# Loading and turning the gate row, the second key weights and the warm-up at the start of a gated attention/MLP kernel

## The chip, the cores and the metric

The kernel runs on one core of a Trainium2 chip. Times are device microseconds of one execution. A NeuronCore has five engines with a queue each: TensorE (PE, matmuls; PEld is its weight load), VectorE (DVE), ScalarE (ACT), GpSimd (POOL) and SyncE (SP). ACT, POOL and SP also issue loads and stores, which 16 DMA engines carry out.

## What is computed

For a sequence of 2048 tokens of width 576, a gate mixes a linear attention block with an MLP:

```python
x = A_x
g = _sigmoid((x * gate_w).sum(-1, keepdims=True))
a = _A_ref(x, A_wqkv, A_wo)      # 32 heads of 18; phi(t) = where(t > 0, t + 1, exp(t)) + 1e-6
b = _B_ref(x, B_w1, B_b1, B_w2, B_b2)   # layernorm, 4608 wide GELU MLP
return g * a + (1 - g) * b
```

In `_A_ref`, queries, keys and values are projections of x; phi of keys and values are summed over the sequence per head, and phi of the queries reads that sum.

## The kernel before

All matmuls keep fp32 precision by splitting each operand into a hi part (rounded to the matmul type, written by ACT with a Copy) and a low part (what is left, a subtraction on DVE), and adding the products of hi and low. The 2048 tokens lie in 16 blocks of 128. Attention comes first (some 290 us), then the MLP in chunks.

The change lies in the start, which prepares the first three blocks. PE first runs `WARM` fp32 matmuls of a tile of ones into bank 7 (line 152; each becomes two instructions). The loads are written in a fixed order (lines 430 to 444): `load_x` brings a transposed block of x by SP, one load of 256 KB and two of 32 KB; `load_w` brings one of the four halves (key or query, first or second 288 columns) of the projection weights, five pieces of 128 rows, the first four together as a main load and the fifth (64 rows) twice, as the tail. The first half of the key weights is issued by ACT in three loads, its tail by SP; everything after by SP. ACT also issues two loads of the gate row `gw`.

A half projection (`first_keys`, `first_queries`) is 14 matmuls in the order `HI_FIRST`: four hi by hi, four low x by hi weights, the two of the tail, four hi x by low weights. `split_x` and `split_w` write the parts. The gate row must become a column: five one-row transposes with the identity `ident` into bank 7 (`column`), and a DVE copy into column 288 of the second key weights, which have 290 columns: those weights' projection then also gives the gate's sum and x's own sum. So the second key weights can be split only after that copy. `make_identity` and the memset and selections of `mask` run on POOL, the former before all loads. `InOrder` makes each engine keep the order of the program; the program has eight semaphores for the loads of SP and ACT, so a ninth issue waits until an earlier load has landed.

The projections of keys go to banks 0 to 5, those of queries in turn to banks 6 and 7, so the third half projection of queries waits until DVE has read the first out of its bank (`phi`).

Of the kernel before, what the change touches and what calls it, by code (L numbers as in the profile page):

```python
# [17 lines left out]
P = 128  # L18
S, D, H, DH, F = 2048, 576, 32, 18, 4608
# [14 lines left out]
MOMENTS = ((0, 2), (2, 4), (4, 8), (8, 16))  # L34
EPS_PHI = 1e-6
EPS_LN = 1e-5
WARM = 6
FIRST = 3
LATE = 3
X_RING = 4  # L40
# [43 lines left out]
def raw(ap):  # L84
    return ap.bitcast(F32)
# [26 lines left out]
def tile_gated_mix(ctx: ExitStack, tc: tile.TileContext, x, xm, xe, wm, we, wvm, wve, wo, um, ue, w2, b1, b2, gw, out):  # L112
    nc = tc.nc
    pe, act, dve, pool = (InOrder(tc, e) for e in (nc.tensor, nc.scalar, nc.vector, nc.gpsimd))
# [17 lines left out]
    def load_twice(dst, src, by=sp):  # L132
        for half in range(2):
            by.dma_start(dst[half * 64:(half + 1) * 64], src)
# [15 lines left out]
    for n in range(4):  # L150
        dve.memset(low_rows[32 * n:32 * n + 32], -1.0 if n % 2 else 0.0)
    for _ in range(WARM):
        pe.matmul(ps[:, 7, :P], ones, ones, start=True, stop=True)
# [3 lines left out]
    accs = keep.tile([P, 7 * TPB * HALF], F32, name="accs")  # L157
    spare = accs[:, :7 * TPB * HALF - TPS * D]
    ident = spare[:, 25 * P:26 * P]
    make_identity(nc, ident)  # L160
    mask = spare[:GW, 26 * P:26 * P + GW]
    acc = [accs[:, spare.shape[1] + i * D:][:, :D] for i in range(TPS)]
    acc += [accrp.tile([P, D], F32, name=f"acc{i}") for i in range(TPS, NT)]
# [20 lines left out]
    QUERY, KEY = range(2)  # L184
    W, at_ = {}, 0
    for part in (KEY, QUERY):
        for half in range(2):
            n = HALF + 2 * (part == KEY and half)
# [17 lines left out]
    def load_w(part, half, pieces=((0, 5),), by=sp):  # L206
        if (part, half) not in wraw:
            wraw[part, half] = wsp.tile([P, 5, HALF + 2], F32, name="s", tag="s")
        s = wraw[part, half]
        main = wm[part * 2 + half].rearrange("p (t n) -> p t n", t=4)  # L210
        tail = we[part * 2 + half]
        for t0, t1 in pieces:
            if t0 < 4:
                by.dma_start(s[:, t0:min(t1, 4), :HALF], main[:, t0:min(t1, 4)])
            if t1 == 5:
                load_twice(s[:, 4, :HALF], tail, by)

    def split_w(part, half, by=dve, pieces=((0, 5),)):
        w = W[part, half]
        s = wraw[part, half][:, :, :w.shape[2]]  # L220
        for t0, t1 in pieces:
            act.activation(w[:, t0:t1], s[:, t0:t1], AF.Copy)
            by.tensor_tensor(out=w[:, 5 + t0:5 + t1], in0=s[:, t0:t1], in1=raw(w[:, t0:t1]), op=OP.subtract)

    def load_x(i):
        xraw[i] = yt.tile([P, 5, P], F32, name="t")
        sp.dma_start(xraw[i][:, 0:4], xm[i].rearrange("p (t n) -> p t n", t=4))
        load_twice(xraw[i][:, 4], xe[i])

    def split_x(i, pieces=((0, 5),)):  # L230
        if i not in xs:
            xs[i] = x_places[PLACE[i] % X_RING]
        to, src = xs[i], xraw[i]
        for t0, t1 in pieces:
            act.activation(to[:, t0:t1], src[:, t0:t1], AF.Copy)
            if t0 < 4:
                dve.tensor_sub(to[:, 5:9], src[:, 0:4], raw(to[:, 0:4]))
            if t1 == 5:
                dve.tensor_sub(to[64:P, 4], src[64:P, 4], raw(to[64:P, 4]))
# [12 lines left out]
    def project(i, part, half, order=BY_ROWS, n=None):  # L252
        w = W[part, half]
        p = banks[i, part, half] = ps[:, next(halves_in) if n is None else n]
        for m, (a, b) in enumerate(order):
            pe.matmul(p[:, :w.shape[2]], xs[i][:, a, :], w[:, b], start=(m == 0), stop=(m == len(order) - 1))
# [173 lines left out]
    first = ORDER[:FIRST]  # L430
    gwr = spare[0:1, :5 * P]
    load_x(first[0])
    load_w(KEY, 0, ((0, 1), (1, 2), (2, 4)), act)
    act.dma_start(gwr[:, :D], gw.rearrange("(a n) -> a n", a=1))
    act.dma_start(gwr[:, D:], gw[4 * P:D].rearrange("(a n) -> a n", a=1))
    act.activation(tiny, ones[:, 0:1], AF.Exp)
    load_w(KEY, 0, ((4, 5),))
    load_x(first[1])
    load_w(KEY, 1)
    load_x(first[2])  # L440
    load_w(QUERY, 0)
    load_xn(first[0])
# [13 lines left out]
    def first_keys(n, half):  # L456
        project(first[n], KEY, half, HI_FIRST, 3 * half + n)
# [7 lines left out]


    column = ps[:, 7, :5]
    for t in range(5):
        pe.transpose(column[:, t:t + 1], gwr[:, t * P:(t + 1) * P], ident[0:1, 0:1])
    first_keys(0, 0)  # L470
    split_x(first[1])
    first_keys(1, 0)
    dve.tensor_copy(wraw[KEY, 1][:, :, HALF:HALF + 1], column[:, :, None])
    dve.memset(wraw[KEY, 1][:, :, HALF + 1:HALF + 2], 1.0)
    split_w(KEY, 1)
    split_x(first[2])
    load_x(ORDER[3])
    first_keys(0, 1)
# [729 lines left out]
```

## Time and profile before

| | us |
|---|---|
| runs without profile | 1133.76, 1134.5, 1137.68 |
| median of these | 1134.5 |
| the profiled execution | 1137.47 |
| its span, first to last instruction | 1135.8 |
| PE busy in the span | 1118.9 (99%) |
| DVE busy | 884.3 (78%) |
| ACT busy | 527.5 (46%) |
| POOL busy | 303.8 (27%) |
| mean granted TensorE clock | 0.997 |

The page gives busy times of one execution. A matmul's time is from its start to its modelled end, and neighbours overlap; the distance of two starts is the pace. "Idle before" names what ended an idle stretch of an engine. A name with q (SPq, ACTq) is the queue of an engine, where it issues DMAs.

### The profile page before, as it was taken

Reading aid. Unit: us, or ns where it says so; the run is one execution under the profiler, and the core shown is the slowest. Engines: PE = TensorE matmul, PEld = TensorE weight load, DVE = VectorE, ACT = ScalarE, POOL = GpSimd, SP = SyncE. Lnnn points to the kernel's source line nnn. Section 1 sums busy time; section 2 is a strip of 40 time slices with the busy share of each in tenths; the row PEclk is TensorE's granted clock in tenths of the full one; section 3 lists DMA queues with packets and bytes.
Section 4 is the critical chain, followed back from the end, with each engine's and each line's share of the span. In section 5 each row is a group of like instructions: output and inputs, shape, how many; then the busy total and the mean of one; then the engine's idle time right before and its main releaser. Section 6 shows DMA issues by size and latency. Waiting matters only on the chain.

```text
span 1135.8 us, 18099 instructions
## 1 busy us (share of the span) xinstructions
PE 1118.9 (99%) x6871; PEld 1025.1 (90%) x6871; DVE 884.3 (78%) x1354; ACT 527.5 (46%) x889; POOL 303.8 (27%) x245
## 2 busy tenths in 40 slices
PE   8999899999999999999999999999999999999998
PEld 8999899999899999999999999988999899989988
DVE  6678787798468878769778766578889888888985
ACT  4555354353545545444544544364445444544441
POOL 1011112242013122212113211234353435343520
PEclk9999899999999999999999999999999999999999
DMA  5237555334454664563764639844444444444452
GB/s 172 68 109 261 163 173 184 141 131 172 171 176 143 230 215 169 204 198 130 255 225 139 230 131 368 316 123 148 117 123 132 139 126 119 139 129 126 126 183 84
DMA packets 102861, 189.85 MB, mean 167 GB/s; under 512 B 8159, under 2 KB 58623, under 8 KB 98550
## 3 DMA queue, kind: packets, MB, share of 16 engines
q1 hardware_dynamic: 102210, 188.10, 50.4%
q8 instruction: 54, 0.88, 0.3%
q10 hardware_dynamic: 564, 0.59, 0.1%
q14 instruction: 33, 0.27, 0.1%
HBM read 121.93 MB, written 66.73 MB: 166 GB/s over the span
## 4 chain that ended last, share of the span: by engine, by line
PE 88%; DVE 6%; ACT 2%; issue 1%; DMA 1%; SPq 0%; DVEq 0%; ACTq 0%
PE ps L108 88%; DVE den L108 1%; DVE accs L108 1%; DVE qt L108 1%; DMA t<-in_xm 1%; DVE acc L108 0%; DMA yd<-ys 0%; DVE y L108 0%; DVE u L108 0%; ACT y L108 0%; DVE e L108 0%; DMA s<-in_wm 0%; DVE region L108 0%; DVE ys L108 0%; ACT h L108 0%
## 5 line engine op out<-in xcount | busy, mean ns | idle before, releaser
L108 PEld LDWEIGHTS ps<-region,h 128*128 128x128 f32 x2568 | 368.5, 188 | 22.6 <-DVE accs L108 1.0
L108 PE MATMUL ps<-region,h 128*128 128x288 f32 x2568 | 383.2, 295 | 0.5 <-DVE fresh L108 0.2
L108 PE MATMUL ps<-y,wa 128*128 128x512 f32 x1008 | 265.0, 392 | 0.0
L108 POOL TENSOR_TENSOR fresh<-fresh 128x384 f32<-128x384 f32 (+1 forms) x128 | 138.1, 1084 | 438.5 <-DMA w1d<-wb 125.9
L108 PE MATMUL ps<-y,wb 128*128 128x512 f32 x756 | 201.1, 395 | 1.0 <-ACT u L108 1.0
L108 PEld LDWEIGHTS ps<-y,wa 128*128 128x128 f32 x1008 | 177.8, 188 | 26.2
L108 DVE TENSOR_TENSOR accs<-ps,accs 128x576 f32<-128x576 f32 x210 | 158.0, 753 | 32.6 <-PE ps L108 22.9
L108 ACT ACTIVATE h<-u,b1s 128x512 fp32r<-128x512 f32 x90 | 65.2, 725 | 214.7 <-DVE u L108 214.7
L108 PEld LDWEIGHTS ps<-y,wb 128*128 128x128 f32 x756 | 132.9, 188 | 23.2 <-ACT u L108 1.7
L108 DVE SCALAR_TENSOR_TENSOR accs<-ps,omg,accs 128x576 f32<-128x576 f32 (+1 forms) x146 | 118.1, 809 | 44.0 <-PE ps L108 43.2
L108 POOL TENSOR_TENSOR u<-u 128x512 f32<-128x512 f32 x64 | 100.2, 1566 | 126.4 <-ACT u L108 122.7
L108 ACT ACTIVATE u<-ps 128x512 f32<-128x512 f32 x108 | 63.7, 590 | 150.0 <-PE ps L108 149.7
L108 PE MATMUL ps<-y 128*128 128x288 f32 (+1 forms) x896 | 128.9, 302 | 1.1 <-ACT y L108 0.4
L108 PEld LDWEIGHTS ps<-y 128*128 128x128 f32 x896 | 125.8, 193 | 3.7 <-ACT y L108 0.9
L108 DVE TENSOR_TENSOR h<-u,h 128x512 fp32r<-128x512 f32 x142 | 104.9, 738 | 27.2 <-ACT u L108 27.1
L108 ACT ACTIVATE u<-u,b1s 128x512 f32<-128x512 f32 x108 | 78.3, 725 | 54.0 <-DVE u L108 51.0
L108 DVE TENSOR_TENSOR u<-ps,u 128x512 f32<-128x512 f32 x108 | 74.2, 687 | 37.1 <-ACT u L108 23.8
L108 PEld LDWEIGHTS ps<-region 128*128 128x128 f32 x600 | 90.3, 188 | 9.0 <-ACT accs L108 0.5
L108 DVE TENSOR_TENSOR region<-fresh,region 128x576 fp32r<-128x576 f32 (+1 forms) x83 | 80.8, 973 | 20.6 <-ACT region L108 20.6
L108 PE MATMUL ps<-region 128*128 128x288 f32 x600 | 96.2, 295 | 0.1
L108 PE MATMUL ps<-wp,qt 128*128 128x288 f32 x448 | 63.6, 298 | 0.8 <-DVE qt L108 0.8
L108 PEld LDWEIGHTS ps<-wp,qt 128*128 128x128 f32 x448 | 59.9, 188 | 1.3 <-DVE qt L108 1.3
(131 smaller groups left out, 1045.8 us busy)
## 6 DMA issues: line engine op xcount, KB each, us to landing
w1d<-wa SPq DMA_DIRECT2D x18, 1280.0 KB
wa<-w1d SPq DMA_DIRECT2D x72, 320.0 KB
y<-yd SPq DMA_DIRECT2D x14, 1280.0 KB
w1d<-wb SPq DMA_DIRECT2D x18, 960.0 KB
wb<-w1d SPq DMA_DIRECT2D x54, 320.0 KB
fresh<-in_w SPq DMA_DIRECT2D x20, 576.0 KB
fresh<-in_w SPq DMA_DIRECT2D x32, 288.0 KB
fresh<-in_um SPq DMA_DIRECT2D x64, 128.0 KB
```

The source lines that it names most:

```text
L108: return lambda *args, **kwargs: self.tc.keep_in_program_order(op(*args, **kwargs))
```

## The change

`WARM` goes from 6 to 11. ACT issues, instead of the two loads of the gate row, the main load of the second key weights. POOL issues the gate row's two loads and the two tail loads of the second key weights; SP no longer issues these weights. `make_identity` is moved behind the loads of the second x block, on POOL behind its four loads. The five transposes of the gate row stand behind the first half projection instead of ahead of it. The second key weights are split in two pieces, the four main ones and the tail.

```diff
-WARM = 6
+WARM = 11
...
-    make_identity(nc, ident)
...
     load_w(KEY, 0, ((0, 1), (1, 2), (2, 4)), act)
-    act.dma_start(gwr[:, :D], gw.rearrange("(a n) -> a n", a=1))
-    act.dma_start(gwr[:, D:], gw[4 * P:D].rearrange("(a n) -> a n", a=1))
+    load_w(KEY, 1, ((0, 4),), act)
+    pool.dma_start(gwr[:, :D], gw.rearrange("(a n) -> a n", a=1))
+    pool.dma_start(gwr[:, D:], gw[4 * P:D].rearrange("(a n) -> a n", a=1))
+    load_w(KEY, 1, ((4, 5),), pool)
     act.activation(tiny, ones[:, 0:1], AF.Exp)
     load_w(KEY, 0, ((4, 5),))
     load_x(first[1])
-    load_w(KEY, 1)
+    make_identity(nc, ident)
     load_x(first[2])
...
     column = ps[:, 7, :5]
+    first_keys(0, 0)
+    split_x(first[1])
     for t in range(5):
         pe.transpose(column[:, t:t + 1], gwr[:, t * P:(t + 1) * P], ident[0:1, 0:1])
-    first_keys(0, 0)
-    split_x(first[1])
     first_keys(1, 0)
     dve.tensor_copy(wraw[KEY, 1][:, :, HALF:HALF + 1], column[:, :, None])
     dve.memset(wraw[KEY, 1][:, :, HALF + 1:HALF + 2], 1.0)
-    split_w(KEY, 1)
+    split_w(KEY, 1, pieces=((0, 4), (4, 5)))
```

## Rows read from the trace of the kernel before

**Rows 1.** The page, busy time of PE over the span.

```profile
PE 1118.9 (99%) x6871; PEld 1025.1 (90%) x6871; DVE 884.3 (78%) x1354; ACT 527.5 (46%) x889; POOL 303.8 (27%) x245
```

**Rows 2.** Chain of waits, 0 to 60 us: start, length, what.

```profile
7.87 8.07 PE ps L108 x40
...
25.51 34.61 PE ps L108 x224
```

**Rows 3.** Order of time, ACT, 0 to 17 us: start, length, operation [idle before].

```profile
2.22 2.11 ACTq L108 DMA_DIRECT2D accs<-in_gw  x2
...
4.10 0.23 ACTq L108 DMA_DIRECT2D accs<-in_gw  x1
4.36 1.28 ACT L108 ACT_TABLE_LOAD   x1 [4.36 <-DMA t<-in_xm]
...
5.76 0.61 ACT L108 ACTIVATE y<-t 128x512 fp32r<-128x512 f32 x1
...
7.15 1.00 ACT L108 ACTIVATE y<-s 128x576 fp32r<-128x576 f32 x2
8.40 0.74 ACT L108 ACTIVATE y<-t 128x640 fp32r<-128x640 f32 x1 [0.25 <-DMA t<-in_xe]
11.80 1.42 ACT L108 ACTIVATE y<-s 128x1450 fp32r<-128x1450 f32 x1 [2.65 <-DMA s<-in_we]
...
16.37 1.42 ACT L108 ACTIVATE y<-s 128x1440 fp32r<-128x1440 f32 x1
```

**Rows 4.** Order of time, SP's queue, 5 to 9 us.

```profile
6.62 0.60 SPq L108 DMA_DIRECT2D s<-in_wm  x1
7.26 1.26 SPq L108 DMA_DIRECT2D s<-in_we  x2
```

**Rows 5.** Windows of 1 us: engines' busy time, clock, DMA share, GB/s.

```profile
4.00:5.00 1.00, 0.06 (x1) 0.00 (x0) 0.00 (x0) 0.64 (x1) 0.00 (x0) 1.00 1.08 372
5.00:6.00 1.00, 0.22 (x3) 0.26 (x3) 0.00 (x0) 0.99 (x3) 0.00 (x0) 1.00 0.34 87
...
7.00:8.00 1.00, 0.83 (x3) 0.46 (x3) 0.97 (x4) 1.00 (x4) 0.00 (x0) 1.00 0.40 126
```

**Rows 6.** PE by shape in 8.3:12.8, 22:24.8, 127.5:128.9: count, busy us, mean ns.

```profile
L108 PE MATMUL ps<-y 128*128 128x288 f32 x20 | 5.2, 450 | 0.2 <-ACT y L108 0.2
...
L108 PE MATMUL ps<-y 128*128 128x288 f32 x23 | 3.2, 296 | 0.0
...
L108 PE MATMUL ps<-y 128*128 128x288 f32 x7 | 1.9, 442 | 0.0
```

**Rows 7.** Order of time, PE, 0 to 32 us: warm-up and transposes.

```profile
1.12 2.93 PE L108 MATMUL ps<-ones 128*128 128x128 f32 x12 [1.12 <-DVE ones L108]
5.78 0.71 PE L108 MATMUL ps<-accs 1*128 1x1 f32 x5 [1.72 <-DMA accs<-in_gw]
```

**Rows 8.** Order of time, DVE, 4 to 17 and 20.9 to 27 us.

```profile
9.24 1.00 DVE L108 TENSOR_TENSOR y<-t,y 128x512 fp32r<-128x512 f32 x2
10.27 0.17 DVE L108 COPY s<-ps 128x5 f32<-128x5 f32 x1
...
13.25 1.67 DVE L108 TENSOR_TENSOR y<-s,y 128x1450 fp32r<-128x1450 f32 x1 [2.80 <-ACT y L108]
...
21.83 1.55 DVE L108 TENSOR_SCALAR e<-e 128x288 f32<-128x288 f32 x1
```

**Rows 9.** Order of time, POOL, 0 to 20 us, its first work for a block.

```profile
17.55 0.67 POOL L108 COPY pks<-k 128x576 f32<-128x576 f32 x1 [15.23 <-DVE k L108]
```

**Rows 10.** One window, 122.2 to 129 us; columns as in rows 5.

```profile
122.20:129.00 6.80, 5.63 (x20) 5.25 (x21) 3.44 (x10) 1.41 (x3) 0.00 (x0) 0.50 0.31 74
```

**Rows 11.** Order of time, PE, around 123 and 148 us.

```profile
123.37 0.38 PE L108 MATMUL ps<-accs,mr 128*8 128x128 f32 x1 [3.62 <-DVE acc L108]
123.40 4.03 PE L108 MATMUL ps<-ks,xs 128*128 128x64 f32 x11
...
148.52 2.15 PE L108 MATMUL ps<-ks,xs 128*128 128x64 f32 x11
```

## Prediction of the change

> **What bounds the kernel now.** I read the page first. The profiled execution took 1137.47 us, of which 1135.8 us are span; the other 1.7 us lie outside the instructions. TensorE (PE) is busy for 99% of the span [rows 1], so a microsecond that PE gets back early stays won unless something later absorbs it. The change touches only what is issued in the first microseconds, so the second view was the chain of waits of the first 60 us [rows 2]. It runs over PE from 7.87 for 8.07 us (the first three half projections of keys, 14 matmuls each), then over ScalarE (ACT) and VectorE (DVE) to 25.51, where PE starts the third half projection of queries; from there it is PE alone for 34.61 us. What the change wins is therefore what it takes off 25.51.
>
> The third view was the order of time on each queue. ACT issues three weight loads and a gate-row load, then stands until 4.10 before the second gate-row load, begins its table load at 4.36 and the first split of x at 5.76 [rows 3]. From there to 8.15 it is never idle, so PE's start at 7.87 is set by when ACT starts, not by a load. ACT waits 0.25 us for the second x block (8.40), and 2.65 us for the second key weights (11.80). SP issues those weights late, at 6.62 to 8.52 [rows 4], while the DMA engines are half idle between 5 and 8 us [rows 5].
>
> The fourth view groups PE's matmuls by duration. In 8.3 to 12.8 us the 128x288 matmul has a mean of 450 ns, in 22 to 24.8 us 296 ns, and 442 ns in 127.5 to 128.9 [rows 6]. That last stretch has a granted clock of 0.50 [rows 10]; so the first two half projections run at the lower level (1.2 GHz) too, although the clock column shows 1.00 there. Matmuls overlap, so I count starts: 19 of the first group begin within its 4.5 us, some 240 ns apart, 21 of the second within its 2.8 us, some 135 ns apart.
>
> **The change part by part.** *ACT's queue.* The two gate-row loads leave it, with the stall before the second. In their place comes one load of 576 KB; the same load took SP 0.60 us to issue [rows 4]. ACT issued the first gate load from 2.22 [rows 3], so it is through at 2.82 instead of 4.33, and the table load (1.28 us) and the first split move 1.4 to 1.5 us earlier, to about 4.35. The first x block has landed by then: the wait that ended at 4.36 was for it. The later weight pieces are less sure; ACT never waited for them, so they are bounded only by their use (7.15 for the third piece). I take them to land by about 6.0, which gives back 0.3 us: the hi split of the third piece ends at about 6.7, and PE goes on there instead of at 7.87: 1.1 us earlier.
>
> *Warm-up.* Twelve instructions (six matmuls, two passes each) take 2.93 us [rows 7]; ten more at the 0.21 to 0.23 us of these end at about 6.2 instead of 4.05. They lie beside the loads and hold little back, since the first data comes at about 5.3 and the third weight piece at 6.7. Now PE idles from 4.05 to 5.78 [rows 7] and has gaps until 7.87, and its pace is still the slow one at 12.8 [rows 6]. Without the hole I expect the full clock by 6 to 10 us. Twenty-six matmuls at 135 instead of 240 ns would be worth 2.7 us if nothing else bound them; something does, as follows.
>
> *Gate row behind the first half projection.* Five transposes take 0.71 us of PE on either side [rows 7]. Now they lie in a gap; after, they lie on PE's path between first and second projection, but PE would wait there for the second x block anyway (below), so they cost nothing; without that wait, 0.7 us. Their copy on DVE stands behind the low split of x, as before.
>
> *Second x block, then second key weights.* This is the path that binds. Before: x landed at 8.40, its low split ended on DVE at 10.24, the column copy with its memset at 10.45 [rows 8]; the key weights came at 11.80, their hi split took 1.42 us, their low split ran from 13.25 to 14.92. After: the weights are issued from 2.2 instead of 6.6 and are there by 8 to 9. But x is issued no earlier and now shares the DMA engines with them. Bounds: not delayed at all (8.40), or by all of 576 KB at the 372 GB/s of 4 to 5 us [rows 5], 1.55 us. I take 0.3 us, near the low end, since 5 to 6 us is nearly empty (87 GB/s) and most of the weights fit before x is moved. Then low split of x until 10.55, column until 10.75, hi split of four of five pieces 1.17 us (1160 columns between the 0.43 us of 288 and the 1.42 us of 1450) until 11.9, low splits 1.36 and 0.45 us until 13.7, against 14.92. PE has used the eight products that need hi parts alone and has six left (0.8 us): the third half projection ends at about 14.5 instead of 15.94. Gain 1.2 (by DVE) to 1.4 us (by PE); I take **1.3 us**.
>
> *Splitting in two pieces* costs ACT 0.18 us and DVE 0.14 us more, and is in that sum.
>
> *From there to 25.51* nothing is changed. The split of the query weights started at 16.37 without a wait [rows 3], so they may be the next to be late; but SP now issues 1.86 us less ahead of them (0.60 and 1.26) [rows 4], more than the 1.3 us that they are wanted earlier. PE itself needs five half projections, 9.4 us, from 14.4 to 23.8: under 24.2, so DVE's chain still sets it and the 1.3 us hold.
>
> *GpSimd (POOL)* gets two gate loads and two 72 KB loads, ahead of the identity and the mask. It has nothing else to do until 17.55 [rows 9]. No row shows a load issued by POOL. Nearest rows: 0.23 us for a gate load [rows 3], 0.63 us for each half of a weight tail [rows 4], together 1.7 us; even at twice that, its few mask ops end soon after DVE's splits have begun. Beside them DVE could be held up: the 0.30 us op that took 1.55 us at 21.83 beside a POOL add shows how [rows 8]. Bounds 0 to 1.2 us; I take 0, since most of it lies ahead.
>
> Sum: 1135.8 - 1.3 = 1134.5 us span, 1136.2 us with the part outside, for an execution like the profiled one. The runs without profile took 1133.76, 1134.5 and 1137.68; against their median the forecast is 1134.5 - 1.3 = **1133.2 us**. Bounds of this case: gain 0.3 (POOL beside DVE, x later) to 1.9 us (x not later, clock early), 1132.6 to 1134.2.
>
> **The rivals.** *The clock falls at 122 us: the other side.* After a stretch of 3.62 us in which PE waits for DVE, the granted clock is 0.50 from 122.2 to 129.0 [rows 10, 11]. The eleven sums of products behind the wait take 4.03 us, and 2.15 us at 148.52 where the clock is full; until 129.0 the projection that follows runs 1.6 us at half pace, another 0.8. Together 2.7 us. The times shown lie in two pairs, 1133.8 and 1134.5, 1137.5 and 1137.7, 3.0 to 3.9 us apart; I read the upper pair as executions in which the clock fell here, as it did in the profiled one. The change neither removes nor lengthens that wait. If the median of after is such an execution it is 1133.2 + 3.0 = 1136.2 us, slower than the median of before. It decides once two of three have it; two of the four shown do.
>
> *The second key weights are paid for by x.* The DMA engines finish them before x: 1.55 us late, x at 9.95, column at 12.3, low split at 15.2: 0.3 us later than before, 1134.8 us. For it: at 4 to 5 us the share is full [rows 5]. Against it: 0.34 and 0.40 later [rows 5]. The Trainium skill speaks for this rival (DMA: Bandwidth & Descriptors, "Issuing engines are not separate DMA queues"): loads of several engines interleave on the same 16 DMA engines, and issuing from more of them saves issue time alone. By that the move is worth no bandwidth; the idle share in this trace says that issue time was what was missing.
>
> *The change doesn't do what it says: the pace doubles no earlier.* Then 26 matmuls at 240 ns from 6.75 and the transposes end at about 13.7, PE starts the third half projection where it does now, and only the wait for the low part goes, 0.3 us: 1134.2 us. For: no row shows PE's clock rising in a warm-up. Against: it rose by 13.8 after some five unbroken microseconds of matmuls.
>
> *POOL's loads come late.* ACT takes the tail of the second key weights before the third x block and every exponential, so all wait for it. It is wanted at 11.9; from 13.2 on the gain is gone, from 16.6 on the kernel is 0.3% slower; at 17 it takes 1138.3 us. For: no row has a load of POOL. Against: SP's pair was used 4.5 us after its issue behind a full queue [rows 3, 4], and POOL issues from about 0.8 us on. The Trainium skill adds (SBUF — State Buffer, "SBUF: two separate sides") that POOL cannot write descriptors while DVE holds the port that both share; no run here shows it.
>
> **How the numbers follow.** Differences up to 0.3% (3.4 us: 1131.1 to 1137.9) can't be told from no change here. Forecast 0.46, clock falling in the median run 0.34, x paying 0.07, no earlier clock 0.06, POOL late 0.04, a gain of over 3.4 us by something unseen 0.03. The range 1131.8 to 1136.9 holds the forecast with its bounds and most of the second case, whose bounds are wider by the spread of the upper pair. POOL's case, and a falling clock without any gain, pass 1137.9: slower 0.05; faster 0.04; within 0.3% 0.91. The forecast's own range is 1132.6 to 1134.2.
>
> **What would show it.** Right: table load at about 2.9; PE's first projection going on at 6.7, with starts 135 ns apart by 10 us; the second x block split at 8.4 to 9.2; the second key weights' low part done by 13.7; the third half projection of queries at 24.0 to 24.5 instead of 25.51; the same order and lengths after. Wrong: starts 240 ns apart until 13 us (no clock), the x split after 9.5 (loads in each other's way), ACT waiting for a POOL load, or DVE ops stretched beside POOL's masks. A time near 1136 with the clock at 0.50 near 120 us is the second case.

## The result, and the profile after

| us | before | after |
|---|---|---|
| runs (14 each) | 1133.76 to 1137.68, median 1135.4 | 1135.39 to 1140.92, median 1138.99 |
| the profiled execution, its span | 1137.47, 1135.8 | 1139.82, 1138.1 |
| PE starts the third half projection of queries | 25.51 | 29.04 |

After over before is 1.0027, 95% interval 1.0019 to 1.0036: some 3 us slower. The forecast was 1.3 us faster, and the range ended at 1136.9.

ACT in order of time: start, length, operation, and in brackets the idle time before it and what ended it.

```profile
0.81 2.04 ACTq L108 DMA_DIRECT2D s<-in_wm  x4
2.88 1.28 ACT L108 ACT_TABLE_LOAD   x1 [2.88 <-issue]
...
4.29 0.61 ACT L108 ACTIVATE y<-t 128x512 fp32r<-128x512 f32 x1
4.81 0.76 ACT L108 ACTIVATE y<-s 128x288 fp32r<-128x288 f32 x2
7.46 0.31 ACT L108 ACTIVATE y<-t 128x128 fp32r<-128x128 f32 x1 [1.89 <-DMA t<-in_xe]
7.68 0.67 ACT L108 ACTIVATE y<-s 128x576 fp32r<-128x576 f32 x1
10.49 0.44 ACT L108 ACTIVATE y<-s 128x288 fp32r<-128x288 f32 x1 [2.15 <-DMA s<-in_we]
11.61 0.74 ACT L108 ACTIVATE y<-t 128x640 fp32r<-128x640 f32 x1 [0.67 <-DMA t<-in_xe]
13.92 1.51 ACT L108 ACTIVATE y<-s 128x1160 fp32r<-128x1160 f32 x2 [1.58 <-DVE s L108]
```

Against [rows 3]: the table load and the first split come 1.5 us earlier, at 2.88 and 4.29. From 5.6 on ACT stands, which before it did not until 8.15, and three times for a load that SP issued: the tail of the first x block (7.46), the tail of the first key weights (10.49), the second x block (11.61; 8.40 before). At 13.92 it waits for VectorE, whose column copy has waited for PE's transposes. PE shows what that does:

```profile
1.13 4.31 PE L108 MATMUL ps<-ones 128*128 128x128 f32 x22 [1.13 <-DVE ones L108]
5.29 0.73 PE L108 MATMUL ps<-y 128*128 128x288 f32 x2
8.39 1.81 PE L108 MATMUL ps<-y 128*128 128x288 f32 x6 [2.38 <-ACT y L108]
10.99 2.06 PE L108 MATMUL ps<-y 128*128 128x288 f32 x6 [0.79 <-ACT y L108]
12.98 0.69 PE L108 MATMUL ps<-accs 1*128 1x1 f32 x5
```

After the warm-up two matmuls run, then PE is idle for 2.38 us. The third half projection of queries stands in the chain of waits of after, as in [rows 2]:

```profile
28.52 0.47 DVE accs L108
...
29.04 31.02 PE ps L108 x200
```

Windows of after: length, busy time (instructions) of PE, PEld, DVE, ACT, POOL, then granted clock, DMA share, GB/s.

```profile
5.00:6.00 1.00, 1.00 (x6) 0.62 (x5) 1.00 (x3) 0.57 (x2) 0.11 (x1) 1.00 1.05 267
6.00:7.00 1.00, 0.02 (x1) 0.00 (x0) 0.36 (x1) 0.00 (x0) 0.00 (x0) 1.00 1.07 242
...
8.00:18.10 10.10, 8.92 (x36) 8.07 (x37) 5.38 (x12) 3.95 (x7) 0.00 (x0) 0.50 0.94 266
```

The pace of the warm-up doubled at 4.5 us; in the hole the granted clock fell to 0.50 (1.2 GHz), and it stayed there from 7.91 to 18.15. All but the first two matmuls of the first two half projections ran at it. And the DMA engines are full. Before, [rows 5] show them at 0.34 in 5 to 6 us and at 0.40 in 7 to 8; the window between, which is not among those rows, has 0.76:

```profile
6.00:7.00 1.00, 0.72 (x6) 0.64 (x5) 0.59 (x1) 1.00 (x4) 0.00 (x0) 1.00 0.76 209
```

By queue (packets, MB, share), 5 to 8 us of after; q10 is ACT's queue, q1 SP's, q0 POOL's:

```profile
q10 hardware_dynamic: 476, 0.53, 73.3%
q0 software_dynamic: 60, 0.13, 17.5%
q1 hardware_dynamic: 120, 0.11, 16.3%
```

Before, SP's queue had this stretch to itself, and moved 0.42 MB. Now ACT's load of 576 KB takes most of it, and SP gets 0.11 MB of 0.77, though SP's loads of the first weights' tail and of x are waiting all the time (issued from 2.52 and 4.64). A share of the same kind, a quarter (0.09 of 0.37 MB), could have been read in the trace of before, at 4 to 5 us, where ACT's load of the first weights is under way:

```profile
q10 hardware_dynamic: 260, 0.28, 79.0%
q1 hardware_dynamic: 142, 0.09, 29.4%
```

From 29.04 to the end the profiled execution of after takes 1.2 us less than that of before, in two places that other kernels here show too: around 125 us its clock is at 0.50 for 3.4 us and not for 6.8 [rows 10] (1.06 us), and a stretch behind 240 us is 0.26 us shorter (both below).

### The profile page after: what moved, and what is told of

It is laid out like the page before. It is cut to its first block, busy times and chain, and to the rows that moved or that the text cites. A ratio compares the mean times of both kernels' runs of the same rounds, so it can differ in the third digit from the quotient of the medians.

```text
span 1138.1 us, 18129 instructions
## 1 busy us (share of the span) xinstructions
PE 1120.4 (98%) x6881; PEld 1026.4 (90%) x6881; DVE 883.7 (78%) x1355; ACT 527.9 (46%) x890; POOL 306.0 (27%) x249
## 4 chain that ended last, share of the span: by engine, by line
PE 86%; DVE 7%; ACT 2%; issue 2%; DMA 2%; SPq 1%; ACTq 0%; DVEq 0%
PE ps L108 86%; DVE accs L108 1%; DVE den L108 1%; DMA s<-in_wm 1%; DVE qt L108 1%; SPq L108 1%; DVE region L108 1%; DVE acc L108 0%; DVE u L108 0%; DVE e L108 0%; DMA yd<-ys 0%; DVE y L108 0%; ACT L108 0%; DMA t<-in_xe 0%; DVE ys L108 0%
```

## The experiments

The theory: the main load of the second key weights, issued at 2.2 us by ACT, crowds SP's small loads; these open a hole in PE's work, and the clock falls in it. Rivals: POOL's loads or the longer warm-up do the harm; the queue that issues does it, not the time. All edits are to the changed kernel, where not said otherwise. "Distance" is the mean of the runs less that of the kernel before run beside them, in us; its 95% interval reaches some 1.0 to either side (1.5 in b2), as the ratio's does, and the two columns differ by up to 0.6 us. "Mark" is PE's start of the third half projection of queries. The three columns of starts come from one profiled execution of each kernel: b1 and d1, which start alike, agree within 0.05 us, before and e1 within 0.2, after and e2 only within 1.1. In the text a kernel is called by the first two characters of its name.

| kernel | first tail split | second x split | mark | ratio, 95% | distance |
|---|---|---|---|---|---|
| before | 7.72 | 8.40 | 25.51 | | |
| after | 10.49 | 11.61 | 29.04 | 1.0027 [1.0019, 1.0036] | +2.97 |
| a1_k1_by_sp | 7.26 | 8.18 | 24.74 | 0.9997 [0.9988, 1.0006] | -0.13 |
| b1_main_by_sp | 7.44 | 8.26 | 23.95 | 0.9999 [0.9990, 1.0008] | +0.35 |
| c1_all_sp | 6.77 | 7.86 | 25.73 | 0.9991 [0.9982, 1.0001] | -0.43 |
| b2_half_on_act | 8.61 | 9.66 | 25.23 | 1.0009 [0.9995, 1.0022] | +1.32 |
| d4_main_later_on_act | 7.14 | 9.83 | 25.40 | 1.0012 [1.0003, 1.0022] | +1.28 |
| a2_no_pool | 8.69 | 9.77 | 27.31 | 1.0004 [0.9993, 1.0015] | +0.55 |
| d3_tail_by_sp | 8.25 | 9.49 | 25.06 | 0.9991 [0.9982, 1.0000] | -0.70 |
| b3_tail_first | 8.89 | 9.22 | 26.45 | 1.0015 [1.0006, 1.0025] | +1.95 |
| a3_warm24 | 9.93 | 11.08 | 26.65 | 0.9999 [0.9989, 1.0008] | +0.08 |
| d2_warm6 | 10.14 | 11.24 | 29.36 | 1.0027 [1.0017, 1.0036] | +2.83 |
| a4_before_warm11 | 7.62 | 9.24 | 25.40 | 0.9998 [0.9988, 1.0008] | -0.62 |
| d1_main_by_sp_sum_later | 7.48 | 8.31 | 23.91 | 0.9984 [0.9976, 0.9993] | -1.55 |
| e1_before_sum_later | 7.81 | 8.40 | 25.71 | 0.9991 [0.9982, 1.0000] | -0.74 |
| e2_after_sum_later | 9.65 | 10.94 | 27.92 | 1.0018 [1.0010, 1.0027] | +1.83 |

### Who issues the second key weights, and when

**All of them by SP behind the second x block**, the gate row by POOL:

```diff
-    load_w(KEY, 1, ((0, 4),), act)
...
-    load_w(KEY, 1, ((4, 5),), pool)
...
     load_x(first[1])
+    load_w(KEY, 1)
```

> The changed kernel, but the second key weights are issued by SP again, behind the second x block as before the change; gate row on POOL, transposes behind the first half projection, 11 warm-up matmuls and the split in two pieces stay. Mark: start of the third half projection of queries, 25.5 us before the change, 29.0 after it. Crowding theory (the 576 KB that ACT issues at 2.2 us take the DMA engines from the first weights' tail and the second x block): tail split by 7.5, x split at 8.4 to 9, mark at 24.0 to 25.2, time 0.3 to 1.5 us under the kernel before. POOL theory (any load from POOL's queue holds up all others): the two gate-row loads stay on POOL, so the tail and x are still about 1 us late, mark at 26 or later. Clock theory (the loss is PE's clock falling in the hole behind a warm-up that ends early): the hole gets short with the loads in time, so it expects what crowding expects.

The loss is gone, and the mark is 0.8 us ahead of that of before; the gain in time that was expected, 0.3 to 1.5 us, does not show (-0.13). The longer warm-up, the gate row on POOL, the later transposes and the split in two pieces are all still in this kernel, so none of them alone is the loss. **Only the main load by SP**, POOL keeps the tail:

> The changed kernel, but the main load of the second key weights (576 KB) is issued by SP behind the second x block; their tail (2 x 72 KB) and the gate row stay on POOL, issued from 1.4 us. Marks: first weights' tail split on ACT (7.7 us before, 10.5 changed, 8.7 without POOL loads, 7.3 with all key weights on SP), third half projection of queries (25.5, 29.0, 27.3, 24.7). Main-load theory (the 576 KB on ACT are what crowds): tail split by 7.6, mark at 24.5 to 25.2. POOL theory (the two tail loads of 72 KB from POOL cost the 1.8 us that lay between the changed kernel and the one without POOL loads, whatever the main load does): tail split at 8.5 to 9.5, mark at 26 to 27.

This is the start that the prediction described. VectorE of b1, and PE at the mark:

```profile
9.03 1.01 DVE L108 TENSOR_TENSOR y<-t,y 128x512 fp32r<-128x512 f32 x2 [0.33 <-ACT y L108]
10.12 0.17 DVE L108 COPY s<-ps 128x5 f32<-128x5 f32 x1
...
11.63 1.74 DVE L108 TENSOR_TENSOR y<-s,y 128x1160 fp32r<-128x1160 f32 x2 [1.34 <-ACT y L108]
...
23.95 2.13 PE L108 MATMUL ps<-y 128*128 128x288 f32 x14 [0.21 <-DVE accs L108]
```

The low part of the second key weights is done at 13.4 (forecast 13.7), the mark at 23.95 (24.0 to 24.5). POOL's tail loads do little here: the first tail is split at 7.44, against 7.26 in a1, where SP issues them behind x. **Nothing on POOL**, gate row and key weights by SP behind x:

```diff
-    load_w(KEY, 1, ((0, 4),), act)
-    pool.dma_start(gwr[:, :D], gw.rearrange("(a n) -> a n", a=1))
-    pool.dma_start(gwr[:, D:], gw[4 * P:D].rearrange("(a n) -> a n", a=1))
-    load_w(KEY, 1, ((4, 5),), pool)
...
     load_x(first[1])
+    sp.dma_start(gwr[:, :D], gw.rearrange("(a n) -> a n", a=1))
+    sp.dma_start(gwr[:, D:], gw[4 * P:D].rearrange("(a n) -> a n", a=1))
+    load_w(KEY, 1)
```

> The changed kernel with no load on POOL and none of the second key weights on ACT: SP issues the gate row and then all second key weights behind the second x block (ACT's queue keeps the three loads of the first weights alone; 11 warm-up matmuls, transposes behind the first half projection and the split in two stay). Crowding theory: first weights' tail by 7, x by 8.3, second key weights some 0.7 us later than with the gate row on POOL (11.2), so mark (third half projection of queries) at 24.5 to 25.3 and a time 0 to 1 us under the kernel before. A theory that POOL's gate row itself delays others: mark at 24.0 or less.

x comes earliest of all (7.86), yet the mark is at 25.73, later than the 24.5 to 25.3 expected: the gate row's and the tail's loads on SP push the query weights, whose split waits until 16.84.

```profile
16.84 1.42 ACT L108 ACTIVATE y<-s 128x1440 fp32r<-128x1440 f32 x1 [1.30 <-DMA s<-in_we]
```

**Half on each**, pieces 0 and 1 by ACT, 2 and 3 by SP behind x:

```diff
-    load_w(KEY, 1, ((0, 4),), act)
+    load_w(KEY, 1, ((0, 2),), act)
...
     load_x(first[1])
+    load_w(KEY, 1, ((2, 4),))
```

> The changed kernel with only the first two of the four main pieces of the second key weights (288 KB) on ACT at 2.2 us; the other two are issued by SP behind the second x block; gate row and tail stay on POOL. If the delay goes by the bytes queued ahead on ACT, the first weights' tail is split half way between the changed kernel (10.5) and the one with the main load on SP (7.3 to 9), at about 9, and the mark (third half projection of queries) is at 26 to 27.5. If it is a matter of any load in that place, tail at 10 or later and mark at 28 to 29.

The first tail is split at 7.44, 8.61 and 10.49 (9.65 in e2) with none, half and all of the load on ACT at 2.2 us: the delay grows with the bytes. The mark, at 25.23, is ahead of the 26 to 27.5 expected: in this execution the clock is up from 4.24 and does not fall. **Issued by ACT, later**: behind the split of the first two weight pieces, at 4.82 to 5.47.

```diff
-    load_w(KEY, 1, ((0, 4),), act)
...
     split_w(KEY, 0, pieces=((0, 1), (1, 2)))
+    load_w(KEY, 1, ((0, 4),), act)
```

> The changed kernel with the main load of the second key weights still issued by ACT, but behind the split of the first two weight pieces, at some 5.5 us instead of 2.2. Theory (it is the time of the load that did the harm, since SP's small loads share the DMA engines with it, and not the queue that issues it): first weights' tail split at 7.3 to 7.8 us, x split at 8.2 to 8.8, third half projection of queries at 24.0 to 25.0, median within 1 us of before. Rival (a load on ACT's queue starves SP's whenever it is issued, or ACT's issue delays its splits): x split after 9.5 us, third half projection of queries after 26.

```profile
4.82 0.65 ACTq L108 DMA_DIRECT2D s<-in_wm  x1
6.23 0.31 ACT L108 ACTIVATE y<-t 128x128 fp32r<-128x128 f32 x1 [1.00 <-DMA t<-in_xe]
6.50 1.08 ACT L108 ACTIVATE y<-s 128x576 fp32r<-128x576 f32 x2
9.83 0.74 ACT L108 ACTIVATE y<-t 128x640 fp32r<-128x640 f32 x1 [2.25 <-DMA t<-in_xe]
```

Half right. The first tail is free of harm (7.14), as the theory had it; x, whose loads now lie beside the main load, comes at 9.83, 1.43 us later than before, which was the rival's number (its mark, after 26, was not: 25.40). In 5 to 8 us SP's queue moved 0.44 MB and ACT's 0.32. So when a load is issued decides whom it delays, and neither place on ACT's queue gained time (+2.97 and +1.28).

**POOL's loads away, main load on ACT as in the change** (gate row and tail by SP behind x):

> The changed kernel, but POOL issues no load: SP issues the gate row and the tail of the second key weights behind the second x block; the main load of these weights stays on ACT at 2.2 us. Crowding theory: tail of the first weights still used after 9 us, second x block after 10.5, mark (third half projection of queries) at 28 to 29.5, as in the changed kernel. POOL theory: without POOL's queue the tail is there by 7 and x by 9, mark at 24 to 25.5.

**Only POOL's tail loads away**:

```diff
-    load_w(KEY, 1, ((4, 5),), pool)
...
     load_x(first[1])
+    load_w(KEY, 1, ((4, 5),))
```

> The changed kernel with the two tail loads of the second key weights issued by SP behind the second x block; GpSimd keeps the gate row, ACT the main load. Theory (crowding: GpSimd's tail loads take the place of SP's beside the main load): first weights' tail split at 8.5 to 9.0 us, third half projection of queries at 27.0 to 28.0, median 0 to 1.5 us above before. Rival (GpSimd's tail loads are harmless, its gate row is what mattered in the run without GpSimd): tail split at 10.0 to 10.6, third half projection of queries at 28.5 to 29.5, median 2 to 4 us above before.

a2 meets neither of its theories: first tail, x and mark (8.69, 9.77, 27.31) lie between them. In both kernels the first tail comes earlier than in after, by 1.8 and 2.2 us (1.0 and 1.4 against e2), so POOL's 144 KB, beside the main load, cost SP some 1 to 2 us; without the main load beside them they cost 0.2 (b1 and a1). Between the two kernels the loads differ by 0.3 to 0.4 us, and the clock: in a2 it is at 0.50 from 10.3 to 17.1, in d3 it does not fall at the start, and the mark is at 27.31 and 25.06. One window of each, a2 first:

```profile
10.40:16.00 5.60, 5.60 (x26) 5.30 (x25) 4.10 (x9) 2.53 (x5) 0.00 (x0) 0.50 0.85 233
...
10.40:16.00 5.60, 5.18 (x37) 4.69 (x37) 4.20 (x10) 2.94 (x8) 0.00 (x0) 1.00 0.84 234
```

d3's mark came 2 us ahead of the range expected, and I put that down to the clock. **First weights' tail on ACT ahead of the main load**:

```diff
+    load_w(KEY, 0, ((4, 5),), act)
     load_w(KEY, 1, ((0, 4),), act)
...
-    load_w(KEY, 0, ((4, 5),))
```

> The changed kernel with the tail of the first key weights issued by ACT ahead of the main load of the second, instead of by SP. Crowding theory, by order in the queue: the tail is now ahead of the 576 KB and is split as soon as the third piece is, by 7.5; x, still on SP, stays late (10 to 11.5), so PE has a hole behind the first half projection instead of inside it and the mark (third half projection of queries) is at 27 to 28.5. If order in one queue doesn't matter, tail at 9 or later and mark at 29.

This does not test the order in one queue. It is one load more than the program has semaphores for at that point, so ACT stands from 2.80 to 4.35 before it issues on; the main load goes out at 4.86 and the table load begins at 5.53. First tail, x and mark (8.89, 9.22, 26.45) all lie outside what was expected.

### Warm-up and clock

```diff
-WARM = 11
+WARM = 24
```

> The changed kernel with 24 instead of 11 warm-up matmuls, so that the warm-up reaches to about 8 us and PE has no hole from 5.9 to 8.4. Crowding theory: the loads stay where they are (tail of the first weights split at 10.5, x at 11.6), the granted clock stays at 1.00, and the mark (third half projection of queries) moves from 29.0 to about 27.2: 1.8 of the 3.5 us were the clock's, the rest the loads'. Clock theory: mark at 25.5 or earlier, all of the 3.5 us were the clock's.

The loads are late as in after and e2 (9.93, 11.08), but PE is never idle before 9.4 us, the clock is up from 6.74 and stays until 122 us, and the mark is at 26.65. One window, and PE at the mark:

```profile
8.00:9.50 1.50, 1.50 (x15) 1.50 (x14) 0.00 (x0) 0.00 (x0) 0.00 (x0) 1.00 1.09 239
...
26.65 2.12 PE L108 MATMUL ps<-y 128*128 128x288 f32 x14 [0.25 <-DVE accs L108]
```

So of the 3.5 us that after loses by the mark, some 2.4 go with the clock and 1.1 with the loads alone; against e2, whose clock fell for 6.8 us and not for 10.2, it is 1.3. By the runs, most of the loss goes with the clock: a3 lies 0.08 us from before, after 2.97, though the interval of 1.0 leaves room for the 1.1 by the mark. The runs of a single kernel part in the same way. After has a mean granted clock of 0.994 or 0.995 in twelve of fourteen runs (1136.67 to 1140.92 us) and of 0.997 in two (1135.39 and 1135.71, about the median of before). b2 has 0.994 or 0.995 in four of ten (1138.16 to 1139.05) and 0.997 or 0.998 in six (1134.11 to 1136.63). Only a profiled execution shows where the clock fell; that of after has 0.994. `WARM = 6`, the other way:

> The changed kernel with the old warm-up of 6. Theory (the crowded loads open a hole of some 2 to 3 us in PE's work, the clock falls in it or does not rise at all, and the longer warm-up of the change bought nothing because of this): PE at half pace through its first two half projections as in the changed kernel, the first weights' tail split at 10.0 to 10.6 us, third half projection of queries at 28.5 to 29.5, median 2 to 4 us above before. Rival (the warm-up itself does the harm, by holding PE or by making the clock fall): third half projection of queries below 27.5 us, median within 1 us of before.

Without the longer warm-up the clock rises only at 19.33 and the change loses the same (+2.83): in the change as made the warm-up bought nothing. In the kernel **before**, `WARM = 11` alone:

> The kernel before with 11 instead of 6 warm-up matmuls, nothing else. Crowding theory and the prediction's own step: the clock rises by 6 to 10 us, but the second key weights still come at 11.8 and their low part is ready at 14.9, so the mark (third half projection of queries) moves from 25.5 only to 25.2 to 25.5, time within 0.5 us of the kernel before. Clock theory: 26 matmuls at 135 instead of 240 ns, mark at 23 to 24, time 1.5 to 2.5 us less.

The clock rises at 10.5, not at 12.9 or later, and the mark moves by 0.1 us (distance -0.62, within its interval): there VectorE's chain binds, as the prediction had it.

### Where a gain at the start goes

b1's mark is 1.56 us ahead of that of before, and its runs are no faster. PE's starts along the same matmuls differ between kernels in two places. One is the stretch after PE's 3.6 us wait near 120 us, with the clock at 0.50 for 3.4 us or for 6.8 (50.4 to 50.7 us from the 700th to the 1000th matmul, or 51.4 to 51.7). The other is at 240 us, where VectorE has an operation of 32 columns, `den`, and POOL the additions for the first MLP chunk (`accs`). Both in before, then in b1:

```profile
239.99 1.00 DVE L108 TENSOR_SCALAR den<-den 128x32 f32<-128x32 f32 x1
...
239.94 4.55 POOL L108 TENSOR_TENSOR accs<-accs 128x384 f32<-128x384 f32 x4 [3.87 <-DMA b2b<-in_b]
...
237.40 0.57 DVE L108 TENSOR_SCALAR den<-den 128x32 f32<-128x32 f32 x1
...
241.49 1.40 DVE L108 TENSOR_SCALAR den<-den 128x32 f32<-128x32 f32 x1
...
236.92 4.54 POOL L108 TENSOR_TENSOR accs<-accs 128x384 f32<-128x384 f32 x4 [3.44 <-DMA b2b<-in_b]
241.41 2.82 POOL L108 TENSOR_TENSOR qz<-acc,pks 128x576 f32<-128x576 f32 x2
```

The same operation takes 0.18 us in a4, where POOL's first addition starts 0.01 us behind it. Where the addition starts first, by 0.05 us in before and 0.48 in b1, it takes 1.00 and 0.57 us, and it ends some 0.04 us after the addition, in each of the eight kernels where the addition is first (before, after, a1, a3, b1, b2, b3, d4). The Trainium skill (SBUF — State Buffer, "Who interferes with whom") describes a port pair of VectorE and GpSimd that, for operations such as this tensor_scalar, can be held for a whole instruction by whichever starts first, while the other blocks; the traces agree. From the 1300th to the 1900th matmul PE takes 85.6 to 85.9 us where the operation is short, 87.3 to 87.7 where it is stretched (before and after among them). The additions start when a load lands; that the order of the two also varies between executions of one kernel is my reading of the spread of its runs, and no two profiles of one kernel show it. **b1 with the additions one call later**:

```diff
-    extra[5] += [lambda: sum_w1(0), lambda: act.activation(...)]
+    extra[5] += [lambda: act.activation(...)]
+    extra[6] += [lambda: sum_w1(0)]
```

> The changed kernel with the main load of the second key weights issued by SP behind the second x block (as in b1), and GpSimd's sum for the first MLP chunk one call later in the program. Theory (a gain at the start is given back at 240 us, where GpSimd's accumulating adds start just before a 0.18 us op of VectorE and stretch it to 0.6 to 1.0 us): third half projection of queries starts at 23.5 to 24.5 us, the op named den takes 0.2 us at 238 to 240 us, and the median is 1.0 to 1.7 us below b1's distance to the kernel before (b1: +0.4 by the means), so 0.6 to 1.3 us below before. Rival (the gain is lost elsewhere, and the adds cost the same wherever they lie): den is short, another VectorE op beside the later adds is stretched, and the median stays within 0.5 us of before.

```profile
237.32 0.18 DVE L108 TENSOR_SCALAR den<-den 128x32 f32<-128x32 f32 x1
...
241.29 0.18 DVE L108 TENSOR_SCALAR den<-den 128x32 f32<-128x32 f32 x1
...
237.37 1.44 POOL L108 TENSOR_TENSOR qz<-acc,pks 128x576 f32<-128x576 f32 x1 [3.96 <-DVE den L108]
238.76 5.20 POOL L108 TENSOR_TENSOR accs<-accs 128x384 f32<-128x384 f32 x4
```

POOL's product, which VectorE's reduction releases and which starts 0.05 us behind the short operation, now comes first, and the additions behind it. This kernel beats both before and after: median 1134.29, by the ratio 0.16% under before. The same move in the kernel **before** alone, and in the **changed** one alone:

> The kernel before, with GpSimd's sum for the first MLP chunk one call later and nothing else changed. Theory (the op den and GpSimd's adds meet at 240 us whatever happens at the start, and the move takes that away): den takes 0.2 us, the stretch of TensorE's work that holds it (87.3 to 87.7 us where they meet, 85.6 to 85.9 where they don't) takes 85.9, and the median is 0.6 to 1.3 us below before; then the move alone gives most of the 1.6 us of d1, and the start of d1 gives the rest. Rival (the earlier start is what gains 1.6 us in d1): within 0.4 us of before.

> The changed kernel, with GpSimd's sum for the first MLP chunk one call later and nothing else changed. Theory (the loss of the change lies at its start, 3.5 us by the third half projection of queries, and what happens at 240 us is separate from it): third half projection of queries at 28.5 to 29.5 us, den 0.2 us, median 1.5 to 2.5 us above before, some 1 us below the changed kernel. Rival (part of the change's loss is the meeting at 240 us, which its later start brings about): median within 1 us of before.

The stretch is 85.9 and 85.6 us long in them. The move takes 0.7 us off before (no change is at the edge of its interval) and 1.1 off after, both within the uncertainty of the same number; so nothing shows the meeting to be part of the change's effect, and after stays 1.8 us behind. The mark of e2, 27.92, is ahead of the 28.5 to 29.5 expected; its clock fell for 6.8 us. By the distances, the repaired start is worth 0.8 us of d1's 1.55; that difference is within the intervals. At the mark it is 1.8 us (23.91 against 25.71).

## Why the prediction was wrong

**Right.** Table load about 2.9 and first split about 4.35: 2.88 and 4.29. POOL's four loads took 2.24 us of its queue (1.7 estimated); its mask work was over at 5.1 and stretched nothing on VectorE. That VectorE's chain, not PE's pace, set 25.51 before: a4. That a longer warm-up brings the clock up by 6 to 10 us: at 4.5 in after, and at 4.0 to 7.3 in all other kernels with 11 or 24, but for 10.5 in a4. The chain from x to 24.0 to 24.5, once x is in time: b1 and d1, 23.95 and 23.91, just ahead of it.

**The step that failed** is how long SP's loads are held up by the load that moved to ACT. The sum has it as the delay of x under "Second x block, then second key weights": 0.3 us taken, bounds 0 to 1.55; measured 3.21 (8.40 to 11.61). The upper bound took all bytes of the load at the full rate, and assumed that x loses no more than those. Two things were left out. Beside ACT's load and POOL's, SP's queue got a seventh of the bytes in 5 to 8 us; and what waits there is not x alone but, ahead of it, the first block's tails, which had no term in the sum at all. The first weights' tail was split at 10.49, 2.8 us later than before and 3.8 us after the 6.7 at which PE was to go on; in [rows 3] the split of these weights has no wait to warn of it. It is this tail that PE's chain waits for: x, split at 11.61, was late by itself, but PE reached its first product with x only at 13.60, behind the tail and the transposes. The Trainium skill (DMA: Bandwidth & Descriptors, "Queues, rings and completion order") has each DMA engine take turns between the queues that have work for it, a packet of several descriptors at a time. Equal turns need not be equal bytes, and no run here shows what a turn of either queue holds; the trace shows SP with 0.11 of 0.77 MB.

**The second omission** is the clock, and by a3 the larger part of the loss. "Without the hole I expect the full clock" was right with its condition, and the change made the hole: PE's third weight product, forecast at 6.7, came at 8.39, because the wait ahead of it was for the tail of the first x block (7.46). From there PE at half pace is what binds: the tail at 10.49, six matmuls (2.06), transposes (0.69), a half projection of 3.5 us, third half projection at 17.1. So the transposes, costed at nothing, lie on the path here. A smaller step also failed: SP was to issue the query weights 1.86 us sooner, and issued them at 10.20 instead of 10.35, as it waited for earlier loads to land; ACT was not held up by that.

**The rivals.** "The second key weights are paid for by x" had the right place, but in after not the price: x at 9.95 and 1134.8 us, against 11.61 and a median of 1138.99. Its 1.55 us of delay comes near the 1.43 of d4, where x alone meets the load; one run does not show that to be more than chance. It was given 0.07 because the idle share was read as free bandwidth; but idle engines at 5 to 8 us (0.76 busy in the middle) say nothing of 2 to 5 us, where the load was put. "Pace doubles no earlier" came true in effect for another reason, "POOL's loads late" did not (the tail was split without a wait). "The clock falls at 122 us" was no cause: after has the shorter fall there. Nor does that fall cost the 2.7 us worked out: every profile here has 3.4 us at 0.50 there, and those with 6.8 lose 1.0 us more.

## What to carry to other kernels

A load issued early on a second queue is not free because the DMA engines are idle later: ask which small loads on other queues are then still under way, and give each of these a term, those for the very first work above all. Put a large load behind what is needed first, on the same queue if need be (b1, d1). A longer warm-up bought nothing where a hole followed it (after, d2) or where another engine set the time (a4); where it reached to the data (a3) the loss was gone. What it is worth once the loads are in time, no run here separates.

## What was not expected of the hardware

- Beside a load of 576 KB on ACT's queue, SP's small loads got 0.11 of 0.77 MB over 3 us, and 72 KB issued at 4.1 were used at 10.5. Why the share is so uneven in after, and 0.44 to 0.32 the other way in d4, stays open; packet sizes differ, and no run separates that.
- After a warm-up with the clock up, one hole of 2.38 us was followed by 10.2 us at 0.50; in d3, with gaps of 0.92 and 0.83 us between starts, the clock stayed up, and in b2 and d4 with holes of 1.45 and 1.55 us. In a2 it fell at 10.3 behind holes of 0.25 and 1.21. In e2, with the same start as after, it fell at 9.86 for 6.8 us: executions of one start differ in this.
- The clock column reads 1.00 before the first rise, while the pace is the slow one: d2's two first half projections run at 240 ns a matmul under a 1.00.
- A VectorE operation of 0.18 us took up to 1.40 beside GpSimd's, by whichever started first.
